# Four weight pieces reach bf16 inside their transfers instead of through a staging tile and a cast

## The chip, the cores and the metric

The kernel runs on one core of one Trainium2 chip. Its time is the device time of one execution in microseconds (us). Three executions of the kernel before took 511.12, 511.17 and 511.69 us, the median being 511.17 us. One further execution was recorded by the hardware profiler, and all rows shown below come from it.

The core has five engines with a queue of instructions each, which run in the order of the program and meet only at semaphores: PE (TensorE, matrix products; PEld is its loading of weights), DVE (VectorE), ACT (ScalarE), POOL (GpSimd) and SP (SyncE, which here only issues transfers). 16 DMA engines move the data between HBM and the on-chip memory.

## The reference, cut to what matters

The input is a sequence of 4 x 5824 tokens with 256 channels. A gated linear recurrence runs along each sequence, and a feed-forward part follows it:

```python
sig_r, sig_i = sigmoid(r_gate), sigmoid(i_gate)
a = exp(8 * sig_r * log(sigmoid(a_param)))         # decay per token and channel
u = sqrt(max(1 - a*a, 1e-6)) * sig_i * x
h[t] = a[t] * h[t-1] + u[t]                        # within each of the 4 sequences
out = ((h @ w1) * (h @ w2)) @ w3 @ w_out           # w1, w2: 256x1024, w3: 1024x1024, w_out: 1024x256
```

All inputs and the output are float32. The matrix products run in bf16 with float32 sums.

## The kernel before, in words

The 23,296 tokens are cut into 47 chunks: two of 256 tokens, 44 of 512 and one of 256. Channels lie on the 128 partitions in two blocks, tokens along the free dimension. For each chunk the gates are loaded (r, i, x), pass through the activation function (R, I), are turned from token rows to channel rows (V, U) by PE or by a transposing transfer, and become the decay a (d), its square and root (s, q), the gated input (g), the scan (h) and its bf16 copy y (y). Then come the products with the first up weight w1 (step a) and the second up weight w2 (step b), their evacuation and elementwise product (c, m), and the product with the folded weight (D), its evacuation (e) and the store (o).

w3 and w_out meet no nonlinearity between them, so the kernel folds them once into one 1024x256 weight: each of the eight row blocks of w3 is cast to bf16 (Cw3.k), turned by PE (Ftk), copied out of PSUM (Fck), multiplied with the whole of w_out (Fmk), and scaled into the folded weight (Fek).

All weights are float32 in HBM and bf16 on chip. In the kernel before each piece of 512 KB is loaded by SP's queue into a float32 staging tile named wf (step L, line 407), which takes a slot in the rings of tiles of a or nrm, and is cast by an engine (step C, lines 414 and 416) into its bf16 tile: w_sb for w1 and w2 (two pieces each, Lw2.0 being columns 0 to 511 of w2), wo_sb for w_out (two pieces, Lwo.0 being its first four row blocks), w_t for a block of w3. `W_ACT` and `W_DVE` name the pieces that ACT and DVE cast, POOL casts the others. The function `load_w` has a second way already, for the pieces in the set `CASTING`, which is empty in the kernel before: the transfer is issued on POOL's queue (line 404), straight from float32 HBM into the bf16 tile, and it has no step C.

The order of the whole program is written out by hand, in a table of words (`ORDER`). Each word issues one step, and each engine's own order follows from the order of the words. W is a group of filler products on PE which keep its clock up at the start; they are in the table like all else. SP's transfers share eight completion semaphores in turn, so an issue on SP waits for the transfer issued eight before it. Transfers on POOL's queue have semaphores of their own, which order prints as DMASW0, DMASW1 and so on in the order of their issue. Names of rows: thi or i_t is the i gate after its activation; p2 is the step L173 on POOL (1 + tanh), t2 the step L192 (times x, into u_t), U2 the turning of u_t by PE (L200), g2 the step L248 on DVE, h the scan (L270), y the cast of h (L280, L282).

Of the kernel before, what the change touches and what calls it, by code (L numbers as in the profile page):

```python
# [23 lines left out]
def kernel(  # L24
# [74 lines left out]
    W_DVE = {('w1', 1)}  # L99
    STAGE = {'w1': ['a', 'a'], 'w2': ['nrm', 'nrm'], 'w3': ['a', 'nrm', 'a', 'nrm', 'a', 'nrm', 'a', 'nrm'], 'wo':  # L100
        ['a', 'nrm']}
    CASTING = set()
    WARM = [2] * 16
    HALVED = 4
    RINGS = {"r": 4, "i": 5, "x": 4, "th_r": 3, "u": 2, "rt": 2, "ut": 6, "a": 6, "nrm": 6, "h": 2, "y": 4,
# [277 lines left out]
    def piece(nm, i):  # L383
        if nm in ("w1", "w2"):
            cols = slice(i * CT, (i + 1) * CT)
            w_in, w_sb = (moe_w1, w1_sb) if nm == "w1" else (moe_w2, w2_sb)
            return w_in.rearrange("(cb p) f -> p cb f", p=P)[:, :, cols], w_sb[:, :, cols]
        if nm == "wo":
            ks = slice(4 * i, 4 * i + 4)
            return moe_w_out.rearrange("(ko p) f -> p ko f", p=P)[:, ks, :], wo_sb[:, ks, :]  # L390
        return moe_w3[i * P:(i + 1) * P, :].rearrange("p (k f) -> p k f", k=1), None
# [7 lines left out]
    def load_w(nm, i):  # L399
        if (nm, i) in CASTING:  # L400
            dst = piece(nm, i)[1]
            if dst is None:
                T["w3b", i] = dst = ring(ffn, [P, 1, DFF], BF16, name="w3_t", tag="w3")
            nc.gpsimd.dma_start(out=dst, in_=piece(nm, i)[0])
            return
        T["wf", nm, i] = ring(held, [P, NCB, CT], F32, name="wf", tag=STAGE[nm][i])
        nc.sync.dma_start(out=staged(nm, i), in_=piece(nm, i)[0])  # L407
# [66 lines left out]
    def last(c):  # L474
# [18 lines left out]
    }  # L493

    ORDER = """
        r0 i0 x0 Lw1.1 Lw1.0 r2 i2 Lw2.0 Lw3.2 x2 E W13 A3. A0. A1. A2. R0.1 R0.0 W3 W10 V0.0 V0.1 I0 t0.1 d0.0 s0.0
        d0.1 s0.1 q0.0 t0.0 Cw1.1 q0.1 Cw1.0 R2 I2 W5 W8 W0 U0 W4 W11 W6 W12 W7 W9 W2 g0 h0.1 h0.0 y0.1 y0.0 a0.0.1
        a0.1.1 a0.1.0 a0.0.0 V2 W15 Cw2.0 g1 h1.1 h1.0 y1.1 y1.0 d2.1 Lw2.1 Lwo.1 Lwo.0 r3 Cw3.2 d2.0 s2.1 s2.0 q2
        b0.0 c0.0.0 c0.1.0 a1.1.0 m0.0 Ft2 a1.1.1 c1.1.0 b0.1 a1.0.0 a0.2.1 a1.0.1 b1.1 m0.1 Fc2 b1.0 a0.2.0 p2 t2.0
        t2.1 U2 c1.0.0 m1.1 Cw2.1 m1.0 a0.3.1 W14 b0.2 a1.3.1 W1 a1.3.0 c0.2.0 g2 Cwo.1 Cwo.0 r4 Lw3.0 Lw3.5 i3 Lw3.1  # L500
        Lw3.4 x3 Lw3.3 Lw3.6 Lw3.7 r7 m0.2 h2.0 h2.1 R3 a1.2.1 a1.2.0 a0.3.0 c1.3.0 c0.3.0 Fm2 b0.3 b1.2 V3 R4 V4
        c1.2.0 d3.1 d4.0 d3.0 d4.1 m0.3 b1.3 y2 Fe2 m1.2 m1.3 a2.0.0 a2.0.1 b2.0 a2.1.0 c2.0.1 c2.0.0 c2.1.0 m2.0
        Cw3.0 s3.1 Cw3.5 Cw3.1 b2.1 a2.2.1 Ft0 a2.1.1 Fc0 Ft1 c2.1.1 Fc1 s4.0 I3 s4.1 c2.2.1 a2.2.0 Ft5 Fm0 p3 Cw3.4
# [161 lines left out]
```

## Time and profile before

| | kernel before |
|---|---|
| device time, median of 3 | 511.17 us (511.12 to 511.69) |
| profiled execution: span from the first to the last instruction | 509.1 us |
| what lies around that span, against the median | 2.07 us |
| granted TensorE clock | 1.000 |
| PE busy | 501.7 us (99%) |
| ACT / DVE / POOL busy | 461.5 / 431.8 / 318.0 us |
| DMA queues with data | q1 (SP), 123.50 MB; q10, below 0.01 MB |

The page gives no device time of the profiled execution by itself, only its span; sums below are made against the span and carried to the median with the 2.07 us unchanged. "Idle before" in a row is the idle time of that engine just before the row's first instruction, and what released it. A merged row of x4 covers four instructions. PE's rows overlap one another a little, since products are pipelined.

### The profile page before, as it was taken

How to read it: one execution, taken by the hardware profiler on the slowest of the kernel's cores; microseconds unless marked ns; L12 is line 12 of the kernel's file. 1: busy time of each engine (PE TensorE's matmuls, PEld its weight loads, DVE VectorE, ACT ScalarE, POOL GpSimd, SP SyncE). 2: the span in 40 equal slices, each digit the busy share in tenths (PEclk: the TensorE clock that was granted, in tenths of full speed). 3: DMA queues.
4: the chain of work that ended last, by engine and by line, in shares of the span. 5: the costliest groups of instructions: out<-in, count | busy, mean ns of one | idle time of the engine just before them, and what ended most of it. 6: DMA issues, size and time to landing. Idle time of an engine off the chain costs nothing.

```text
span 509.1 us, 8891 instructions
## 1 busy us (share of the span) xinstructions
PE 501.7 (99%) x3225; PEld 308.3 (61%) x3225; DVE 431.8 (85%) x417; ACT 461.5 (91%) x708; POOL 318.0 (62%) x269
## 2 busy tenths in 40 slices
PE   7999999999999999999999999999999999999997
PEld 3767665665665656556656556565566655656566
DVE  6999999999999789879979799878877797959762
ACT  7999999998999999999999999998998979888543
POOL 1686677658658937964886973956647568580200
PEclk9999999999999999999999999999999999999999
DMA  8999999999989998896999997899886895252213
GB/s 317 410 411 345 335 316 282 305 286 259 310 220 298 279 285 247 211 302 196 247 305 327 254 286 148 252 243 227 210 246 164 235 298 161 85 166 62 65 51 104
DMA packets 178048, 124.06 MB, mean 244 GB/s; under 512 B 87378, under 2 KB 174036, under 8 KB 178004
## 3 DMA queue, kind: packets, MB, share of 16 engines
q1 hardware_dynamic: 178000, 123.50, 85.4%
q8 instruction: 25, 0.41, 0.4%
q14 instruction: 19, 0.16, 0.1%
q10 hardware_dynamic: 4, 0.00, 0.0%
HBM read 78.91 MB, written 23.86 MB: 202 GB/s over the span
## 4 chain that ended last, share of the span: by engine, by line
PE 92%; ACT 3%; DMA 2%; POOL 1%; DVE 1%; issue 1%; SPq 1%; ACTq 0%; DVEq 0%
PE po L357 30%; PE pb L299 29%; PE pa L299 29%; DMA wf<-in_moe_w_dram 2%; PE pw L436 1%; ACT sa L322 1%; PE ptr L200 1%; PE ptw L425 1%; POOL u_t L192 0%; DVE h_t L270 0%; SPq L151 0%; ACT ot L322 0%; SPq L407 0%; ACT L168 0%; ACT L238 0%
## 5 line engine op out<-in xcount | busy, mean ns | idle before, releaser
L337 DVE TENSOR_TENSOR g_t<-sa,pb 128x1024 bf16<-128x1024 bf16 (+1 forms) x188 | 218.7, 1180 | 58.9 <-PE pb L299 27.6
L299 PEld LDWEIGHTS <-w_sb 128*128 128x128 bf16 x1504 | 146.4, 98 | 144.1 <-issue 1.4
L322 ACT CAST sa<-pa 128x512 bf16<-128x512 f32 (+1 forms) x332 | 179.8, 591 | 27.1 <-PE pa L299 18.9
L299 PE MATMUL pa<-y_t,w_sb 128*128 128x512 bf16 (+1 forms) x752 | 190.2, 372 | 0.2 <-ACT sa L322 0.2
L299 PE MATMUL pb<-y_t,w_sb 128*128 128x512 bf16 (+1 forms) x752 | 184.9, 372 | 0.2 <-ACT w_sb L414 0.2
L357 PE MATMUL po<-wp_sb,g_t 128*128 128x256 bf16 (+1 forms) x1464 | 177.6, 272 | 0.0
L357 PEld LDWEIGHTS <-g_t 128*128 128x128 bf16 x1464 | 142.5, 98 | 39.5 <-issue 0.3
L282 POOL CAST y_t<-h_t 128x1024 bf16<-128x1024 f32 (+2 forms) x47 | 53.8, 1145 | 140.2 <-DVE h_t L270 136.1
L192 POOL TENSOR_TENSOR u_t<-i_t,x_t 128x512 bf16<-128x512 f32 (+1 forms) x90 | 123.3, 1387 | 3.8 <-DMA ut<-u_t 1.8
L270 DVE TENSOR_TENSOR_SCAN h_t<-a_t,h_t,nrm 128x512 f32<-128x512 f32 (+1 forms) x92 | 121.1, 1343 | 1.6
L233 POOL TENSOR_TENSOR nrm<-a_t 128x512 f32<-128x512 f32 x70 | 78.4, 1137 | 7.0 <-ACT a_t L223 4.0
L223 ACT ACTIVATE a_t<-rt,la 128x512 f32<-128x512 bf16 (+1 forms) x82 | 66.1, 823 | 0.0
L322 ACT COPY ot<-po 128x512 f32<-128x512 f32 x84 | 49.1, 589 | 13.2 <-PE po L357 12.9
L173 POOL TENSOR_SCALAR i_t<-i_t 128x1024 f32<-128x1024 f32 (+1 forms) x45 | 55.4, 1233 | 8.3 <-ACT i_t L168 8.3
L251 DVE SCALAR_TENSOR_TENSOR nrm<-nrm,ut 128x1024 f32<-128x1024 f32 (+1 forms) x39 | 53.2, 1365 | 5.2 <-ACT nrm L238 5.2
L168 ACT ACTIVATE i_t<-i_t 128x1024 f32<-128x1024 f32 (+1 forms) x46 | 48.5, 1063 | 0.3 <-DMA i_t<-in_i_gate_dram 0.2
L238 ACT ACTIVATE nrm<-nrm 128x1024 f32<-128x1024 f32 (+1 forms) x47 | 48.4, 1040 | 0.2
L162 ACT ACTIVATE th_r<-r_t 128x1024 bf16<-128x1024 f32 (+1 forms) x41 | 43.5, 1064 | 0.0
L320 DVE CAST sa<-pa 128x512 bf16<-128x512 f32 x36 | 23.5, 684 | 1.4 <-PE pa L299 0.8
L238 ACT ACT_TABLE_LOAD x17 | 21.8, 1283 | 0.4
L287 PE MATMUL warm<-ident 128*128 128x512 bf16 x32 | 10.7, 473 | 1.6 <-DVE ident L441 1.6
L231 ACT ACTIVATE nrm<-a_t 128x512 f32<-128x512 f32 x18 | 11.4, 645 | 0.0
(55 smaller groups left out, 122.1 us busy)
## 6 DMA issues: line engine op xcount, KB each, us to landing
r_t<-in_r_gate_dram SPq DMA_DIRECT2D x45, 512.0 KB, 5.2
i_t<-in_i_gate_dram SPq DMA_DIRECT2D x45, 512.0 KB, 6.0
x_t<-in_x_dram SPq DMA_DIRECT2D x45, 512.0 KB, 5.5
out_dram<-ot SPq DMA_DIRECT2D x90, 256.0 KB, 3.9
wf<-in_moe_w_dram SPq DMA_DIRECT2D x12, 512.0 KB, 10.5
wf<-in_moe_w_out_dram SPq DMA_DIRECT2D x2, 512.0 KB, 10.2
rt<-th_r SPq DMA_TRANSPOSE x41, 4.7
ut<-u_t SPq DMA_TRANSPOSE x39, 4.4
```

Source lines behind the costliest of these rows:

```text
L173: (nc.vector if c in DV_PLUS else nc.gpsimd).tensor_scalar(t, t, 1.0, 1.0, op0=ALU.add, op1=ALU.mult)
L192: (nc.vector if (c, half) in DV_HALF else nc.gpsimd).tensor_mul(out=u, in0=t, in1=xt)
L223: nc.scalar.activation(out=a, in_=pr, func=AF.Exp, scale=la4[:, cb:cb + 1], bias=la4[:, cb:cb + 1])
L233: (nc.vector if (c, cb) in DV_SQUARE else nc.gpsimd).tensor_mul(out=n, in0=a, in1=a)
L238: nc.scalar.activation(out=n, in_=n, func=AF.Sqrt, scale=-1.0, bias=1.0)
L251: nc.vector.scalar_tensor_tensor(out=n, in0=n, scalar=1e-3, in1=T["pu", c][:, :, cols], op0=ALU.max, op1=ALU.mult)
L270: nc.vector.tensor_tensor_scan(h[:, cb, :], a[:, cb, :], n[:, cb, :], init, ALU.mult, ALU.add)
L282: (nc.vector if key in DV_CAST else nc.gpsimd).tensor_copy(out=y, in_=h)
L299: nc.tensor.matmul(out=dst, lhsT=w_sb[:, cb, m * P:(m + 1) * P], rhs=T["y", gates_of(c)][:, cb, span(c, mp)], start=(cb == 0), stop=(cb == ...
L322: nc.scalar.copy(out=dst, in_=src_ps)
L337: nc.vector.tensor_mul(out=T["g", z][:, 2 * mp:2 * mp + 2, span(c, mp)], in0=T["sa", c, mp][:, :, :w], in1=T["pb", c, mp][:, :, :w])
L357: nc.tensor.matmul(out=po, lhsT=T["g", c][:, k, j * P:(j + 1) * P], rhs=wp_sb[:, k, cols], start=(k == 0), stop=(k == KD - 1), skip_group_ ...
```

## The change

The set `CASTING` now holds both pieces of w2 and both of w_out. Their loads leave SP's queue and are issued by POOL, and the four casts (one on ACT, three on POOL) are gone with their staging tiles. In the table, Lw2.0 moves from its place between i2 and Lw3.2 to a place behind Cw1.0, and the words of the four casts are taken out; Lw2.1, Lwo.1 and Lwo.0 stay where they were.

```diff
-    CASTING = set()
+    CASTING = {('w2', 0), ('w2', 1), ('wo', 0), ('wo', 1)}
...
     ORDER = """
-        r0 i0 x0 Lw1.1 Lw1.0 r2 i2 Lw2.0 Lw3.2 x2 E W13 A3. A0. A1. A2. R0.1 R0.0 W3 W10 V0.0 V0.1 I0 t0.1 d0.0 s0.0
-        d0.1 s0.1 q0.0 t0.0 Cw1.1 q0.1 Cw1.0 R2 I2 W5 W8 W0 U0 W4 W11 W6 W12 W7 W9 W2 g0 h0.1 h0.0 y0.1 y0.0 a0.0.1
-        a0.1.1 a0.1.0 a0.0.0 V2 W15 Cw2.0 g1 h1.1 h1.0 y1.1 y1.0 d2.1 Lw2.1 Lwo.1 Lwo.0 r3 Cw3.2 d2.0 s2.1 s2.0 q2
+        r0 i0 x0 Lw1.1 Lw1.0 r2 i2 Lw3.2 x2 E W13 A3. A0. A1. A2. R0.1 R0.0 W3 W10 V0.0 V0.1 I0 t0.1 d0.0 s0.0
+        d0.1 s0.1 q0.0 t0.0 Cw1.1 q0.1 Cw1.0 Lw2.0 R2 I2 W5 W8 W0 U0 W4 W11 W6 W12 W7 W9 W2 g0 h0.1 h0.0 y0.1 y0.0 a0.0.1
+        a0.1.1 a0.1.0 a0.0.0 V2 W15 g1 h1.1 h1.0 y1.1 y1.0 d2.1 Lw2.1 Lwo.1 Lwo.0 r3 Cw3.2 d2.0 s2.1 s2.0 q2
         b0.0 c0.0.0 c0.1.0 a1.1.0 m0.0 Ft2 a1.1.1 c1.1.0 b0.1 a1.0.0 a0.2.1 a1.0.1 b1.1 m0.1 Fc2 b1.0 a0.2.0 p2 t2.0
-        t2.1 U2 c1.0.0 m1.1 Cw2.1 m1.0 a0.3.1 W14 b0.2 a1.3.1 W1 a1.3.0 c0.2.0 g2 Cwo.1 Cwo.0 r4 Lw3.0 Lw3.5 i3 Lw3.1
+        t2.1 U2 c1.0.0 m1.1 m1.0 a0.3.1 W14 b0.2 a1.3.1 W1 a1.3.0 c0.2.0 g2 r4 Lw3.0 Lw3.5 i3 Lw3.1
```

On POOL, the place is the first stage, from the cast of w1's first piece on. Before, its rows were:

```order
L416 CAST w_sb<-wf 128x2x512
L282 CAST y_t<-h_t 128x256 x2
L416 CAST w_t<-wf 128x1024
L173 TENSOR_SCALAR i_t<-i_t 128x1024
L192 TENSOR_TENSOR u_t<-i_t,x_t 128x512 x2
L416 CAST w_sb<-wf 128x2x512
L416 CAST wo_sb<-wf 128x1024 x2
L282 CAST y_t<-h_t 128x1024
```

And with the change:

```order
L416 CAST w_sb<-wf 128x2x512
L404 DMA w_sb<-in_moe_w_dram 128x2x512
L282 CAST y_t<-h_t 128x256 x2
L404 DMA w_sb<-in_moe_w_dram 128x2x512
L404 DMA wo_sb<-in_moe_w_out_dram 128x4x256 x2
L416 CAST w_t<-wf 128x1024
L173 TENSOR_SCALAR i_t<-i_t 128x1024
L192 TENSOR_TENSOR u_t<-i_t,x_t 128x512 x2
L282 CAST y_t<-h_t 128x1024
```

Three casts behind t2 are gone. One issue now stands ahead of the two casts of chunk 0's y, and three stand ahead of the cast of w3's block 2 (Cw3.2), of p2 and of t2.

On PE the order of rows is the same; what they wait for is not. These are the first product with w2 (b0.0), and the first product with w_out (Fm2):

```order
 L287 MATMUL warm<-ident 128x512
-L299 LDWEIGHTS w_sb [waits Activation_49]
+L299 LDWEIGHTS w_sb [waits DMASW0_49]
 L299 MATMUL pb<-y_t,w_sb 128x256 [waits PE_49]
 L299 LDWEIGHTS w_sb
```

```order
 L299 MATMUL pa<-y_t,w_sb 128x256
-L436 LDWEIGHTS w3t [waits DVE_49]
-L436 MATMUL pw<-wo_sb,w3t 128x256 [waits Pool_49]
+L436 LDWEIGHTS w3t [waits DMASW3_49]
+L436 MATMUL pw<-wo_sb,w3t 128x256 [waits DVE_49]
 L436 LDWEIGHTS w3t
```

b0.0 waits for the landing of the first transfer on POOL's queue where it waited for ACT's cast, and Fm2 for the fourth (w_out's first half) where it waited for POOL's cast.

On SP, four loads leave the early part of the queue:

```order
 L151 DMA i_t<-in_i_gate_dram 128x1024
-L407 DMA wf<-in_moe_w_dram 128x2x512
 L407 DMA wf<-in_moe_w_dram 128x1024
 L151 DMA x_t<-in_x_dram 128x1024
-L407 DMA wf<-in_moe_w_dram 128x2x512
-L407 DMA wf<-in_moe_w_out_dram 128x4x256 x2
 L151 DMA r_t<-in_r_gate_dram 128x1024 x2
```

The load of w3's block 2 and that of chunk 2's x now stand one load further ahead, all that follows four loads further.

## The prediction

> **What bounds the kernel now.** I read three views in this order: the page's shares, the busy time by stage, and the chain of waits at the start. The page makes PE the bound, but an average doesn't say whether a late start is caught up again, so the table by stage comes next. Its columns are the stretch, its length, then busy time and count of PE, PEld, DVE, ACT and POOL, the granted clock, the DMA share and GB/s:
>
> ```profile
> PE 501.7 (99%) x3225; PEld 308.3 (61%) x3225; DVE 431.8 (85%) x417; ACT 461.5 (91%) x708; POOL 318.0 (62%) x269
> ...
> 14.00:15.22 1.22, 1.03 (x13) 0.54 (x10) 1.22 (x3) 1.10 (x2) 0.00 (x0) 1.00 1.00 408
> 15.22:22.00 6.78, 5.89 (x56) 4.61 (x57) 5.99 (x11) 6.74 (x9) 6.54 (x7) 1.00 1.06 402
> 22.00:495.30 473.30, 473.11 (x3006) 288.69 (x3005) 411.90 (x373) 438.38 (x674) 308.69 (x254) 1.00 0.87 243
> ```
>
> From 22 us to 495 us PE stands idle for 473.30 - 473.11 = 0.19 us. Whatever reaches PE late before 22 us therefore moves the end by the same amount, and nothing behind has room to give it back; nor can work saved on ACT or POOL there help. The change works before 22 us only: there PE's idle time from 14 us on is 0.19 + 0.89 = 1.08 us, and that is all that can be won. The rows of PE say where it lies (start, length, engine, line, what, and in brackets the idle time before it); POOL's follow:
>
> ```profile
> 15.22 0.61 PE L299 MATMUL pb<-y_t,w_sb 128*128 128x256 bf16 x4 [0.19 <-ACT w_sb L414]
> 15.67 0.38 PE L299 MATMUL pa<-y_t,w_sb 128*128 128x256 bf16 x2
> 16.47 0.62 PE L425 MATMUL ptw<-ident,w_t 128*128 128x128 bf16 x8 [0.43 <-POOL w_t L416]
> 19.34 0.28 PE L200 MATMUL ptr<-ident,u_t 128*128 128x128 bf16 x2
> 20.07 0.51 PE L200 MATMUL ptr<-ident,u_t 128*128 128x128 bf16 x6 [0.46 <-POOL u_t L192]
> 23.04 1.04 PE L436 MATMUL pw<-wo_sb,w3t 128*128 128x256 bf16 x8
> 26.38 1.02 PE L299 MATMUL pa<-y_t,w_sb 128*128 128x512 bf16 x4
> ```
> ```profile
> 10.35 1.04 POOL L416 CAST w_sb<-wf 128x1024 bf16<-128x1024 f32 x1 [9.04 <-DMA wf<-in_moe_w_dram]
> 11.99 1.06 POOL L282 CAST y_t<-h_t 128x256 bf16<-128x256 f32 x2 [0.61 <-DVE h_t L270]
> 15.38 1.04 POOL L416 CAST w_t<-wf 128x1024 bf16<-128x1024 f32 x1 [2.33 <-DMA wf<-in_moe_w_dram]
> 17.52 2.50 POOL L192 TENSOR_TENSOR u_t<-i_t,x_t 128x512 bf16<-128x512 f32 x2
> 19.97 1.03 POOL L416 CAST w_sb<-wf 128x1024 bf16<-128x1024 f32 x1
> 20.95 2.02 POOL L416 CAST wo_sb<-wf 128x1024 bf16<-128x1024 f32 x2
> 25.28 1.04 POOL L282 CAST y_t<-h_t 128x1024 bf16<-128x1024 f32 x1 [2.32 <-DVE h_t L270]
> ```
>
> PE's waits at 15.22, 16.47 and 20.07 all end with a cast of weights or with POOL. The chain of waits (start, length, what) names one path for the last two:
>
> ```profile
> 4.66 10.66 DMA wf<-in_moe_w_dram
> 15.32 0.05 issue
> 15.38 1.04 POOL w_t L416
> 16.42 1.03 POOL i_t L173
> 17.45 0.07 issue
> 17.52 2.51 POOL u_t L192 x2
> 20.03 0.05 issue
> 20.07 0.51 PE ptr L200 x6
> 20.58 0.22 PE pa L299 x2
> ```
>
> So the start is set by POOL: the load of w3's block 2 lands at 15.32, then Cw3.2, p2 and t2 run back to back to 20.03, and PE goes on at 20.07. Ahead of that, POOL is idle twice, for 0.61 and for 2.33 us, together 2.94 us. The change puts four issues into these gaps.
>
> **What goes, and what it is worth.** Three POOL casts, 1.03 and 2.02 us in the rows above, stood behind t2 and before y2 at 25.28, which waited 2.32 us for the scan anyway: removing them is worth nothing there.
>
> ```profile
> 14.12 1.04 ACT L414 CAST w_sb<-wf 128x1024 bf16<-128x1024 f32 x1 [0.22 <-DMA wf<-in_moe_w_dram]
> 20.64 0.59 PE L287 MATMUL warm<-ident 128*128 128x512 bf16 x2
> 21.05 0.56 PEld L299 LDWEIGHTS <-w_sb 128*128 128x128 bf16 x6 [0.31 <-POOL w_sb L416]
> ```
>
> The weight load that waited 0.31 us for w2's second piece did so while PE ran filler products (20.64 to 21.23), so nothing is won there either. ACT's cast of w2.0, 1.04 us, gives way to b0.0's own wait for the transfer; ACT is up to 1.04 us earlier, but what it computes next goes to g2, which waits for U2 too. SP loses four loads. The one row that waited for SP's order is Cw3.2: its load now stands one load further ahead.
>
> **The price of an issue on POOL, g.** No row has a transfer issued by POOL. The nearest are SP's plain loads and its transposing transfers, which write many small pieces (least, median and greatest duration, ns):
>
> ```profile
> L407 SPq DMA_DIRECT2D wf<-in_moe_w_dram x12: 327/368/496, 2.1 to 25.0; - x12
> L211 SPq DMA_TRANSPOSE rt<-th_r x41: 1210/1307/2977, 40.3 to 446.0; - x41
> ```
>
> That bounds g by 0.33 us and 1.31 us. I take 1.0 us, nearer the upper row, since each issue covers 256 or 512 rows of the weights, and what is slow in the upper row is a transfer of many pieces. An issue can't be free of POOL's order, since POOL runs it as an instruction between two casts.
>
> Term A, POOL's order. Cw1.0 ends at 10.35 + 1.04 = 11.39. Then come an issue, the y casts (1.06), three issues, and Cw3.2 to t2's end (20.03 - 15.38 = 4.65). t2 ends at 11.39 + 1.06 + 4.65 + 4g = 17.10 + 4g, against 20.03: a shift of 4g - 2.93. With g = 1.0 it is +1.07 us, with 1.31 +2.31. With 0.33 the formula gives -1.61, but then the landing of w3's block 2 and PE's idle time bound it. Queued behind are Cw3.2, p2 and t2 on POOL, Ft2 and U2 on PE, and g2, the scan and y2. y2 ends at 25.28 + 1.04 = 26.32, just ahead of PE's next products at 26.38: nothing there absorbs it. The y casts of chunk 0 start at 12.39 instead of 11.99; the products behind them are 0.40 us late, less than b0.0 by term B.
>
> Term B, the landing of w2.0. How long does a transfer of 512 KB take from the end of its issue? The first load meets empty engines:
>
> ```profile
> 0.74 0.39 SPq L151 DMA_DIRECT2D r_t<-in_r_gate_dram  x1
> 4.29 1.15 ACT L160 ACTIVATE th_r<-r_t 128x512 bf16<-128x512 f32 x2 [0.81 <-DMA r_t<-in_r_gate_dram]
> wf<-in_moe_w_dram SPq DMA_DIRECT2D x12, 512.0 KB, 10.5
> ```
>
> That is 4.29 - 1.13 = 3.16 us alone. But between 14 and 22 us the engines' share is 1.00 and over, at 408 GB/s, by which 512 KB cost 1.28 us of all engines. The lower bound is the load alone: 11.39 + 1.0 + 3.16 = 15.55. The upper is a transfer that stands behind all that SP has in flight, as SP's weight loads do, 10.5 us: 12.39 + 10.5 = 22.9. I take an equal share between two queues that both hold work, which doubles 1.28: 16.83. b0.0, at 15.22 before, starts at 16.88, 1.66 us late. PE's wait of 0.43 us for Cw3.2 and part of the next then vanish, and Ft2 stands at 17.55 (16.88 + 0.67 for the six products ahead of it: 15.67 - 15.22 = 0.45, and 0.22 for the two by the chain's last row); Cw3.2 ends at 11.39 + 4.0 + 1.06 + 1.04 = 17.49. So B and A meet, and the shift at U2 stays +1.07.
>
> One sentence of the Trainium skill bears on B: DMA: Bandwidth & Descriptors, section Issuing engines are not separate DMA queues, states that transfers of all issuing engines interleave on the same 16 DMA engines, which gives the equal share and not the 22.9; no run so far has two busy queues to show it. Another page of the Trainium skill speaks against the change: SBUF — State Buffer, section SBUF: two separate sides, states that VectorE in a two-port mode, such as a float32 copy within SBUF, keeps GpSimd from writing descriptors. Between 11.39 and 16.45 this trace has one such row on DVE, so by that rule the sum would grow by 0.27 us at most:
>
> ```profile
> 14.50 0.27 DVE L282 CAST y_t<-h_t 128x256 bf16<-128x256 f32 x1
> ```
>
> Term C, the landing of w_out. Fm2 needs the fourth transfer on the queue. At an equal share each of the four takes 2.56 us behind the last, so it lands at 16.83 + 3 x 2.56 = 24.51; alone, 3.16 us after its issue at 16.45, it would be 19.6. Fm2, at 23.04 before, stands at 24.11 by A. It waits 0.45 us more, since PE has no idle time behind to lose: +1.07 + 0.45 = +1.52. w2.1, second on the queue, lands at 19.4, before its use at 22.2.
>
> The sum is 509.1 + 1.5 = 510.6 us of span, and with the 2.07 us around it 512.7 us.
>
> **The rivals.**
>
> Cheap issue. If g is like SP's row, 0.33 to 0.5 us, POOL is no longer late: with 0.4 the issues end at 11.39 + 1.6 + 1.06 = 14.05, the load of w3's block 2 lands one load earlier, 15.32 - 1.28 = 14.04, and t2 ends at 18.7. PE then is held by w2.0 alone, at 11.39 + 0.4 + 3.16 = 14.95 to 16.2 by its share: b0.0 up to 1.0 us late, against 0.89 us of idle time behind it that falls away. With 16.2 it is +0.1, 511.3 us; with 14.95 it is -0.9, 510.3 us. For it: SP's rows. Against it: SP's issue is work for an engine that does nothing else. The Trainium skill, DMA: Bandwidth & Descriptors, section Latency and other measured facts, has about 1 us to the first byte on GpSimd's path and about 0.6 us on SP's; by that ratio SP's 0.33 to 0.5 would be 0.55 to 0.83 us, and term A -0.7 to +0.4, an estimate.
>
> Price by rows. If an issue costs by the rows it names, w2's 256 at 1.0 us and w_out's 512 at 2.0, the four take 6.0 us and A is 17.10 + 6.0 - 20.03 = +3.1: 514.2 us. The landings are then later by less than that. For it: the transposing transfers at 1.31 against 0.37 us. Against it: a load's issue of 512 KB shows no such growth on SP.
>
> Late landing. Transfers on POOL's queue come behind SP's backlog, or move slower because they convert. Then B decides, from a landing of about 17 us on: at 22.9 b0.0 is 7.7 us late, less 0.89 of idle time, +6.8: 518.0 us. For it: DMA engines full at 14 us. Against it: the queues are separate, and SP issues no more than eight transfers ahead.
>
> That the new transfers don't convert, or that the casts remain, is excluded: the order of rows shows four issues and four casts fewer.
>
> **How the numbers follow.** Forecast (+0.9 to +2.4) 0.40; price by rows (+2.4 to +5) 0.21; late landing 0.08; cheap issue 0.31, of which 0.06 reach below 510.1, since the idle time to be won is only 1.08 us. The measurement can tell 0.2%, here 1.02 us, from no change: slower is 0.36 of the forecast, the two dear rivals, and 0.01 of the cheap one, together 0.66; the same 0.28; faster 0.06. The range takes in g from about 0.5 us and issues by rows with a slow share: 510.5 to 516.5. It leaves out the far end of the late landing and the best of the cheap issue.
>
> **What would show it.** POOL's rows: y casts of chunk 0 at 12.4, Cw3.2 starting at 16.45 without a wait for its load, t2 ending at 21.1. PE: b0.0 waiting for w_sb until 16.9, U2 for u_t until 21.15, Fm2 for wo_sb until about 24.5, and again no idle time from there to 495 us. If Cw3.2 starts before 15.4, the issue was cheap and A is wrong; if it starts past 18, it goes by rows; if b0.0 waits past 17.5 while POOL is in time, it is the landing. A shift at U2 that the end does not show would make the first step wrong, that nothing behind 22 us gives time back.

## The result, and the profile after

The changed kernel takes 527.25 us (median of 4, 526.99 to 527.93) beside 511.38 us for the kernel before (511.12 to 511.69): a ratio of 1.0313, 95% interval 1.0298 to 1.0327. It is slower by 15.9 us, where the prediction had 512.7 us and a range that ended at 516.5. The profiled execution took 527.13 us with a span of 525.3 us, 16.2 us more than the span before.

The table of stages, in the same columns as before:

```profile
15.22:22.00 6.78, 2.14 (x14) 1.44 (x13) 3.45 (x5) 5.13 (x7) 4.95 (x5) 0.67 1.10 335
29.05:37.06 8.01, 0.02 (x1) 0.00 (x0) 2.01 (x2) 2.22 (x4) 2.02 (x2) 0.63 1.12 356
37.06:42.26 5.20, 5.20 (x36) 4.17 (x37) 1.62 (x3) 0.66 (x1) 0.00 (x0) 0.58 1.05 398
42.26:511.50 469.24, 466.16 (x2910) 285.19 (x2963) 407.32 (x366) 434.41 (x669) 305.44 (x251) 1.00 0.84 228
```

PE stands still twice, and around and after each stop the granted clock (the third number from the end) is below 1. From 42.26 us on the kernel is the old one: the stretch there takes 469.24 us, and the same work before, from the first product at 26.38 us to 495.30, took 468.92. (PE's busy time there looks 3.1 us short of the stretch, but the trace holds 2910 products where the one before held 2961, so records are missing.) The tail behind it is 13.8 us in both. So the whole loss arises before 42.26 us. PE's rows name the two stops:

```profile
20.19 1.03 PE L299 MATMUL pb<-y_t,w_sb 128*128 128x256 bf16 x4 [4.64 <-DMA w_sb<-in_moe_w_dram]
28.03 1.04 PE L299 MATMUL pa<-y_t,w_sb 128*128 128x256 bf16 x8
37.06 1.89 PE L436 MATMUL pw<-wo_sb,w3t 128*128 128x256 bf16 x8 [7.99 <-DMA wo_sb<-in_moe_w_out_dram]
42.26 1.03 PE L299 MATMUL pa<-y_t,w_sb 128*128 128x512 bf16 x3
```

The first product with w2 waits for its transfer until 20.19 (15.22 before), the first with w_out until 37.06 (23.04 before). At 42.26 the same product stands that stood at 26.38. The 16.2 us divide so: PE reaches the end of the products ahead of Fm2 at 37.06 - 7.99 = 29.07 instead of 23.04, 6.0 us late through w2; then 8.0 us of waiting for w_out; then the products from Fm2 on take 5.20 us instead of 3.34 (26.38 - 23.04), 1.9 us; and 0.3 us behind. These are the parts of PE's path and not separate causes: Fm2 starts when w_out has landed at 37.0, and PE's first 6.0 us only shorten its wait for that. POOL, on which the sum rested, is nearly in time:

```profile
11.26 0.93 POOL L404 DMA_DIRECT2D w_sb<-in_moe_w_dram  x1
12.36 1.05 POOL L282 CAST y_t<-h_t 128x256 bf16<-128x256 f32 x2 [0.18 <-DVE h_t L270]
13.35 0.72 POOL L404 DMA_DIRECT2D w_sb<-in_moe_w_dram  x1
14.07 1.51 POOL L404 DMA_DIRECT2D wo_sb<-in_moe_w_out_dram  x2
15.55 1.07 POOL L416 CAST w_t<-wf 128x1024 bf16<-128x1024 f32 x1
17.77 2.48 POOL L192 TENSOR_TENSOR u_t<-i_t,x_t 128x512 bf16<-128x512 f32 x2
```

The issues take 0.93, 0.72 and twice 0.76 us, and t2 ends at 20.25 us, 0.2 us later than before. What is late is the transfers, not their issue. The view of the DMA queues shows why, for 16 to 18 us and for 26 to 28 us (packets, MB as written, busy share of the 16 engines):

```profile
q1 hardware_dynamic: 142, 0.52, 68.7%
q0 software_dynamic: 144, 0.15, 43.2%
...
q1 hardware_dynamic: 165, 0.61, 82.0%
q0 software_dynamic: 164, 0.08, 30.4%
```

q1 is SP's queue, q0 POOL's. In each stretch both queues move the same number of packets: 142 and 144, 165 and 164. But a packet of SP's carries 0.52 MB / 142 = 3.7 KB, one of POOL's 1.0 KB written (a row of 2 KB of w2, converted), and with w_out 0.5 KB (a row of 1 KB). The engines take turns packet by packet, so POOL's queue gets half of the turns and, counted at the source, 0.15 x 2 = 0.3 of 0.8 MB with w2, and 0.16 of 0.77 MB with w_out. A row of w2 has its turn every 2 x 16 / 144 = 0.22 us on each engine, and a piece has 16 rows for each engine: 3.6 us; a piece of w_out has 32, at 0.195 us: 6.2 us. The Trainium skill, DMA: Bandwidth & Descriptors, section Queues, rings and completion order, states the rule, that each engine goes round between the queues by whole packets; these rows agree with it.

### The profile page after: what moved, and what is told of

Same layout as the page of the kernel before. It is cut to its first block, busy times and chain, and to the rows that moved or that the text cites. A ratio compares the mean times of both kernels' runs of the same rounds, so it can differ in the third digit from the quotient of the medians.

```text
span 525.3 us, 8830 instructions
## 1 busy us (share of the span) xinstructions
PE 503.2 (96%) x3170; PEld 311.3 (59%) x3225; DVE 433.6 (83%) x417; ACT 460.7 (88%) x707; POOL 317.9 (61%) x270
## 3 DMA queue, kind: packets, MB, share of 16 engines
q1 hardware_dynamic: 176400, 121.40, 82.4%
## 4 chain that ended last, share of the span: by engine, by line
PE 88%; DMA 5%; ACT 3%; DVE 1%; issue 1%; POOL 0%; SPq 0%; DVEq 0%; ACTq 0%
PE po L357 29%; PE pb L299 29%; PE pa L299 27%; DMA wo_sb<-in_moe_w_out_dram 4%; PE pw L436 2%; ACT sa L322 1%; DMA x_t<-in_x_dram 1%; PE ptr L200 1%; PE ptw L425 1%; DVE h_t L270 1%; ACT ot L322 0%; DVE u_t L189 0%; ACT L168 0%; ACT L238 0%; DVE nrm L233 0%
## 5 line engine op out<-in xcount | busy, mean ns | idle before, releaser
L299 PE MATMUL pa<-y_t,w_sb 128*128 128x512 bf16 (+1 forms) x719 | 186.2, 373 | 1.1 <-ACT sa L322 0.2
L233 POOL TENSOR_TENSOR nrm<-a_t 128x512 f32<-128x512 f32 x70 | 78.4, 1137 | 16.2 <-ACT a_t L223 15.4
L436 PE MATMUL pw<-wo_sb,w3t 128*128 128x256 bf16 x64 | 9.0, 291 | 8.0 <-DMA wo_sb<-in_moe_w_out_dram 8.0
L223 ACT ACTIVATE a_t<-ptr,la 128x512 f32<-128x512 bf16 x10 | 7.2, 774 | 10.4 <-issue 10.3
```

What stands on the lines that cost most here:

```text
L223: nc.scalar.activation(out=a, in_=pr, func=AF.Exp, scale=la4[:, cb:cb + 1], bias=la4[:, cb:cb + 1])
L233: (nc.vector if (c, cb) in DV_SQUARE else nc.gpsimd).tensor_mul(out=n, in0=a, in1=a)
L299: nc.tensor.matmul(out=dst, lhsT=w_sb[:, cb, m * P:(m + 1) * P], rhs=T["y", gates_of(c)][:, cb, span(c, mp)], start=(cb == 0), stop=(cb == ...
```

## The experiments

Theory T is these turns: two queues with work share the engines packet for packet, and what a queue gets in bytes goes by the size of its packets. Its rivals are that converting is slow by itself, that POOL's queue delivers slowly whatever else runs, and that one piece alone is at fault. "Before" was timed beside every run; the ratios below have their 95% interval behind them.

### Which piece costs what

```diff
w2_only
-    CASTING = {('w2', 0), ('w2', 1), ('wo', 0), ('wo', 1)}
+    CASTING = {('w2', 0), ('w2', 1)}          # w_out loaded by SP and cast by POOL as before
wo_only
+    CASTING = {('wo', 0), ('wo', 1)}          # w2 loaded by SP and cast as before
```

> Only the two pieces of w2 are converted in transfers on POOL's queue; w_out is loaded by SP and cast by POOL as before. Theory T (each DMA engine serves the two queues packet by packet, one for one, and POOL's packets are single rows): w2.0 lands at about 20, w2.1 at about 24, as in the changed kernel, Fm2 waits for nothing; PE stays about 6 us late after U2 and the time is about 517 us. Rival C (converting is what is slow, w_out's half included): the same landing of w2. Rival S (one cause only, w_out's late landing, decides, and the wait at b0.0 is absorbed): no change, 511 to 512 us.

> Only the two pieces of w_out are converted in transfers on POOL's queue; w2 is loaded by SP and cast by ACT and POOL as before. Theory T: 64 rows for each engine at one turn in about 0.21 us, from about 15 us on, so the second transfer lands at about 28.5; Fm2 starts there instead of 23.0, and with a lower clock behind the wait the time is 517 to 518 us. Rival S: the whole 16 us come from here, 525 us or more. If the issues alone cost, 512 us.

w2 alone: 515.49 us against 511.21, 1.0084 (1.0067 to 1.0101), +4.3 us. w_out alone: 521.44 us, 1.0204 (1.0187 to 1.0221), +10.2 us. The two don't have to add up to the 15.9 us, since all four transfers stand in one queue. Each piece has its own wait on PE:

```profile
19.36 1.03 PE L299 MATMUL pb<-y_t,w_sb 128*128 128x256 bf16 x4 [4.22 <-DMA w_sb<-in_moe_w_dram]
```
```profile
31.58 1.89 PE L436 MATMUL pw<-wo_sb,w3t 128*128 128x256 bf16 x8 [8.43 <-DMA wo_sb<-in_moe_w_out_dram]
```

The first row is of the kernel with w2 alone, the second of that with w_out alone. Both pieces are at fault, and rival S falls. The sizes were off: w2 costs 1.5 us less than forecast, and w_out lands at 31.5 instead of 28.5, because I let its rows start at 15 us. POOL's queue shows no packet before 17 us there, though its first issue ended at 14.1.

### Is it converting, and is it the queue?

The same four transfers, at the same places on POOL's queue but unconverted, with the casts of before:

```diff
plain_pool (against before; Lw2.0 moved as in the change)
-        nc.sync.dma_start(out=staged(nm, i), in_=piece(nm, i)[0])
+        (nc.gpsimd if nm in ('w2', 'wo') else nc.sync).dma_start(out=staged(nm, i), in_=piece(nm, i)[0])
```

> The same four transfers on POOL's queue at the same places, but not converted: float32 into the staging tiles, cast by ACT and POOL as before. Theory T: packets on POOL's queue stay single rows, the landings are like the changed kernel's (20, 24, 31, 37 us), the casts come on top and stand in POOL's order ahead of y2: 528 us or more. Rival C (converting is what is slow): unconverted transfers get a share by bytes like SP's own, w2.0 lands at 16 to 17, w_out at 24 to 25, and the time is 513 to 516 us.

It takes 517.51 us, 1.0121 (1.0106 to 1.0136): better than the changed kernel, with four casts more. From 20 to 22 us its queues stand so, and over the run q0 has:

```profile
q1 hardware_dynamic: 115, 0.43, 52.9%
q0 software_dynamic: 113, 0.40, 48.9%
```
```profile
q0 software_dynamic: 576, 2.10, 1.0%
```

The turns are one for one again, but the bytes are equal too. 576 packets for 2.10 MB are 3.6 KB each: 512 of them are what packets of 4 KB for each piece and partition give, and the other 64 are 16 for each transfer. So unconverted, POOL's queue joins the rows of one partition (two of w2, four of w_out) into a packet, where the changed kernel has 1600 packets for the same source. So I was wrong that its packets stay single rows, and rival C is right in that converting makes a difference. w2.0 lands at 18.7, w_out's last piece at 27.4, between the two forecasts. PE waits only for the first: b0.0 starts at 19.80. Is converting slow, then, or only its packets small? The next kernel takes SP's packets away:

```diff
quiet (against the change)
+        T["r", 3] = ring(loads, [P, 4, D], F32, name="r_t", tag="r")
+        nc.gpsimd.tensor_copy(out=T["r", 3][:, 0, 0:1], in_=wo_sb[:, 0, 0:1])   # ahead of SP's load r3
```

> The changed kernel, but SP's queue is held: its load of chunk 3's r waits, by one element that POOL copies out of w_out's last piece into that tile, until all four transfers of POOL's queue have landed. SP has then only four loads in flight beside them, and none from about 16 us on. The time means nothing here, the landings do. Theory T (turns): without the other queue's turns a row of w2 takes about 0.10 us of an engine and a row of w_out 0.06, so w2.0 lands by 18 to 19 and w_out's last piece by 23 to 25. Rival L (POOL's queue brings a row each 0.2 us by itself, whatever else runs): 20, 24, 31 and 37 us as in the changed kernel.

From 18 to 20 us only POOL's queue runs, and POOL's copy begins when the last of the four has landed:

```profile
q0 software_dynamic: 738, 0.37, 135.6%
...
20.87 0.19 POOL L420 CAST r_t<-wo_sb 128x1 f32<-128x1 bf16 x1 [5.88 <-DMA wo_sb<-in_moe_w_out_dram]
```

738 packets in 2 us instead of 164, and all landed by 20.9 us instead of 37.0, earlier than the 23 to 25 of the forecast: a row of w_out took 2 x 16 / 738 = 0.043 us of an engine and not 0.06. This kernel ran once, and only its landings are used. Of w_out's rows that is 738 x 1 KB = 0.76 MB of source in 2 us, 378 GB/s, beside the 408 GB/s of plain loads: converting itself is nearly as fast as loading. Rival L falls, and so does slow converting by itself. What is left is the size of its packets beside SP's.

### Longer rows

w2 by row blocks and w_out with eight neighbouring rows on a partition, so that a row of the transfer is 4 KB; the turning of w3 takes its columns in the matching order:

```diff
long_rows (against the change)
+        if nm == "w2":
+            return moe_w2[i * P:(i + 1) * P, :], w2_sb[:, i, :]
-            return moe_w_out.rearrange("(ko p) f -> p ko f", p=P)[:, ks, :], wo_sb[:, ks, :]
+            return moe_w_out.rearrange("(p ko) f -> p ko f", p=P)[:, ks, :], wo_sb[:, ks, :]
-            nc.tensor.matmul(out=pt[:, k, :], lhsT=T["w3b", mi][:, 0, k * P:(k + 1) * P], rhs=ident,
+            nc.tensor.matmul(out=pt[:, k, :], lhsT=T["w3b", mi][:, 0, :].rearrange("p (q k) -> p k q", k=KD)[:, k, :], rhs=ident,
```

> The changed kernel with the same bytes in fewer, longer rows: w2 by row blocks (128 rows of 4 KB a piece, where it was 256 of 2 KB) and w_out with eight neighbouring rows on a partition (128 rows of 4 KB a piece, where it was 512 of 1 KB; the columns of w3 are turned in the matching order). Theory T: 32 turns for each engine in all, where it was 96; b0.0 now needs both pieces of w2, at about 19 to 20; w_out lands by 26, before Fm2 needs it at 28 to 29; 516 to 517 us. Rival C by bytes: the landings stay as they are and b0.0, which needs both pieces, starts at 24: 527 us or more.

518.06 us, 1.0134 (1.0119 to 1.0149): of 15.9 us 9 are gone. The queues from 16 to 18 us, and PE's only waits from there to 45 us:

```profile
q1 hardware_dynamic: 115, 0.44, 57.9%
q0 software_dynamic: 109, 0.19, 50.4%
```
```profile
18.35 0.39 PE L299 MATMUL pb<-y_t,w_sb 128*128 128x256 bf16 x1 [3.30 <-DMA w_sb<-in_moe_w_dram]
20.92 0.82 PE L299 MATMUL pb<-y_t,w_sb 128*128 128x256 bf16 x3 [2.17 <-DMA w_sb<-in_moe_w_dram]
```

0.19 MB written are 0.38 MB of source beside 0.44: with packets of like source size the queues share alike. Fm2 waits no more. What is left is b0.0, which here needs both pieces, the second at 20.9 instead of the 19 to 20 forecast, and the time is 1 us above the 516 to 517 forecast. With w_out alone in long rows (w2 as before):

> Only w_out is converted on POOL's queue, with 128 rows of 4 KB a piece; w2 as before. Theory T: 16 turns for each engine, landed by 21 to 22, before Fm2 at 23.0; the two issues (1.5 us) fit into POOL's idle 2.33 us: 511.2 us, no change. Rival C by bytes: like the run with w_out in short rows.

512.28 us against 511.43, 1.0017 (1.0009 to 1.0026), +0.85 us where +10.2 was the price in short rows. The miss against "no change" is one wait, since w_out lands at 24.0 and not at 21 to 22:

```profile
24.07 1.05 PE L436 MATMUL pw<-wo_sb,w3t 128*128 128x256 bf16 x8 [0.73 <-DMA wo_sb<-in_moe_w_out_dram]
```

Even then there is no gain: the casts saved were covered.

### A second queue that needs no POOL

```diff
plain_act (against before; Lw2.0 moved as in the change)
+        (nc.scalar if nm in ('w2', 'wo') else nc.sync).dma_start(out=staged(nm, i), in_=piece(nm, i)[0])
```

> The same four transfers, unconverted, issued by ACT instead of POOL at the same places, cast as before. Theory T: ACT's queue forms packets of some 3.7 KB as SP's does, so that turns one for one are an equal share of bytes: w2.0 lands at 15 to 17, w_out by 25; 511 to 515 us. If any second queue gets little beside SP's (a rival to the size of packets): landings like the changed kernel's and 525 us or more.

527.89 us, 1.0322 (1.0306 to 1.0339): as slow as the change, and my forecast was wrong by more than 12 us. Its queues from 14 to 16 us and from 28 to 30 us, q10 being ACT's:

```profile
q1 hardware_dynamic: 146, 0.53, 65.1%
q10 hardware_dynamic: 143, 0.29, 38.7%
...
q1 hardware_dynamic: 176, 0.64, 78.5%
q10 hardware_dynamic: 176, 0.18, 25.5%
```

The turns are equal once more. I had taken it that ACT's queue joins rows as I thought SP's did; it does not: its packets are the rows, 2 KB and 1 KB. Nor did SP's queue join them: it has 178,000 packets before and 176,400 in the changed kernel, 1600 fewer for the same four transfers. SP's packets are large in this stage because its rows are (4 KB of w3, and of the r, i and x of chunks 2, 3, 4 and 7). The rival that any second queue gets little has the time right, 525 us or more, but not the cause: in plain_pool POOL's queue got as many bytes as SP's. This kernel is no pure test of the queue, for its issues also stand in ACT's order:

```profile
18.52 3.71 ACTq L407 DMA_DIRECT2D wf<-in_moe_w_out_dram  x2
22.28 0.78 ACT L223 ACTIVATE a_t<-ptr,la 128x512 f32<-128x512 bf16 x1 [3.15 <-DMA wf<-in_moe_w_dram]
```

ACT stands idle for 3.15 us ahead of the row at 22.28, around its second issue of w_out, and the issue of w2.1 comes only at 18.11, behind ACT's cast of w2.0 (on POOL it came at 13.35). So q10 moves 48 packets from 16 to 18 us, none from 18 to 20 and 28 from 20 to 22; at 72 packets per us (143 in 2 us) its queue moved next to nothing for about 4.9 us, an estimate of what ACT's order adds to the landing of w_out at 36.8. The rest of that landing is the turns; no run separates the two.

### The clock

```diff
warm (against the change)
-    WARM = [2] * 16
+    WARM = [2] * 15 + [24, 18, 18]
-        ... a0.3.0 c1.3.0 c0.3.0 Fm2 ...
+        ... a0.3.0 c1.3.0 c0.3.0 W16 W17 Fm2 ...
```

> The changed kernel with filler products on PE where it waits: 22 more ahead of b0.0 (4.7 us) and 36 ahead of Fm2 (7.7 us), sized to end about when the transfers land. Theory: the landings stay, but the granted clock stays at 1.0 through the waits, so the products from 37 to 42 us run at full pace and the time falls by about 2 us to 525 us. Rival (the clock costs nothing, the whole 16 us are waits): no change, or slower by the fillers.

525.02 us, ratio 1.0264 (1.0250 to 1.0278) where the change had 1.0313: 2.2 us less, by products that compute nothing. Behind the landing of w_out, its row and that of the change stand so:

```profile
37.00:42.20 5.20, 5.15 (x45) 3.81 (x46) 3.38 (x6) 2.77 (x5) 1.91 (x2) 1.00 1.05 397
```
```profile
37.06:42.26 5.20, 5.20 (x36) 4.17 (x37) 1.62 (x3) 0.66 (x1) 0.00 (x0) 0.58 1.05 398
```

With fillers the clock is 1.00 and PE issues 45 products in the time of 36. Before the change the same stage, and in the changed kernel the first stretch behind each stop, stand so:

```profile
23.04:26.38 3.34, 3.33 (x39) 2.89 (x37) 3.34 (x5) 3.34 (x7) 1.10 (x2) 1.00 1.02 419
```
```profile
20.19:24.00 3.81, 3.81 (x22) 2.94 (x23) 1.56 (x3) 0.67 (x1) 0.07 (x1) 0.50 1.10 334
37.06:41.00 3.94, 3.94 (x22) 2.96 (x23) 1.09 (x3) 0.00 (x0) 0.00 (x0) 0.50 1.05 404
```

For nearly 4 us behind each stop the clock is half. A wait of PE thus costs more than its length. Behind the first stop the loss is hidden in the wait for w_out, so what the fillers win is the loss behind the second.

### Could the transfers be put elsewhere?

```diff
hold_sp (against the change): ahead of SP's load r3
+        nc.sync.dma_start(out=held_t, in_=wo_sb[0:1, 0, 0:2])
early (against before): Lw2.0 as the first transfer of POOL's queue, the other pieces as before
+    CASTING = {('w2', 0)}
-        r0 i0 x0 Lw1.1 Lw1.0 r2 i2 Lw2.0 Lw3.2 x2 ...
+        Lw2.0 r0 i0 x0 Lw1.1 Lw1.0 r2 i2 Lw3.2 x2 ...
```

> The changed kernel, but SP's queue has one tiny transfer that reads one row of w_out's last piece ahead of its load of chunk 3's r, so that SP issues no more loads until the four transfers of POOL's queue have landed, and no engine but SP waits for that. If turns taken by SP's packets are what made the landings late, w2.0 lands at 16.9 and w_out at 20.4, as when the queue was held by POOL; U2 ends about 1 us later than before the change, Fm2 waits for nothing; but chunk 3's r lands at about 24 instead of 22, so PE gets V3 up to 1.5 us late: 512.5 to 514.5 us in all. If something else made them late, 520 us or more.

> Only w2.0 is converted in a transfer, and it is issued by POOL as its first transfer at about 1 us, where POOL is idle until 10.3; the other three pieces are loaded and cast as before. By turns it lands at 9 to 10 us, ahead of its use at 15.2, so no product waits for it. But its 16 rows for each engine take turns from the loads of chunk 0 (x, w1), which are up to 1.5 us late, and with them the first y; the load of w3's block 2 lands when it did. 511.3 to 512.5 us. If the missing cast on ACT were worth something, 510.3 us or less.

With SP held, w2.0 is there at 16.7 us and Fm2 waits for nothing, as forecast, yet the kernel takes 516.98 us, 1.0105 (1.0090 to 1.0120), above the forecast of at most 514.5. ACT waits 2.11 us for chunk 3's r:

```profile
25.51 1.06 ACT L160 ACTIVATE th_r<-r_t 128x1024 bf16<-128x1024 f32 x1 [2.11 <-DMA r_t<-in_r_gate_dram]
60.00:100.00 40.00, 39.03 (x261) 24.23 (x259) 37.80 (x39) 39.85 (x59) 27.01 (x22) 1.00 1.14 314
```

The load is 1.5 us later than I had it. At the product that stands at 26.38 before, this kernel is 3.1 us late (29.43), but its span is 6.6 us longer (515.7 against 509.1), so half of the loss arises behind this stage. From 60 to 100 us PE loses 0.97 us that it did not lose before, at a DMA share of 1.14 where it was 1.07. I take it that SP's loads had a lead and lost it here; no run shows that. Issued first of all, w2.0 lands 9.2 us after its issue at 1.28, at about 10.5 instead of the 9 to 10 forecast, and no product waits for it. The kernel takes 513.05 us, 1.0031 (1.0018 to 1.0044), +1.4 us and 0.5 above the forecast: chunk 0's x and w1, which share their turns with it, come later, and POOL's cast of w1 starts at 12.30 instead of 10.35. No version tried is faster than the kernel before.

## Why the prediction was wrong, point by point

**That PE's idle time before 22 us bounds a gain, and that nothing behind gives time back**: right. From the same product on, the changed kernel takes 0.3 us more than before, and no kernel tried was faster. Time can still be lost there, as with SP held.

**The price of an issue, 1.0 us** (term A): a little high. It took 0.93 us for the first and 0.72 to 0.76 for the others, 3.2 us for the four instead of 4.0, so t2 ended at 20.25 us instead of 21.1, and the shift from POOL's order was +0.2 us, not +1.07. The rival "price by rows" fell: 512 rows cost no more than 256 (0.76 and 0.72 us; in the kernel with long rows 128 rows took 0.54).

**"I take an equal share between two queues that both hold work, which doubles 1.28: 16.83"** (term B): this is the step that failed. The queues do share equally, but by packets. At 3.7 KB against a converted row a piece of w2 takes 3.6 us and not 2.56, and its first packet comes only some 3.5 us after the end of the issue (12.19 to about 15.7, by the 23 packets that it moved before 16 us), where I had taken 3.16 us from issue to landing without a second queue. w2.0 landed at 20.1, 3.3 us past the value taken, between my bounds of 15.55 and 22.9. It is the case that I had named under what would show it: b0.0 waits past 17.5 while POOL is in time, so it is the landing.

**"Each of the four takes 2.56 us behind the last"** (term C): the same error, larger, since w_out's rows are 1 KB: 6.2 us a piece. Its last piece landed at 37.0 instead of 24.5, and the wait of 0.45 us became 7.99. For this term, which decided, I had worked out no upper bound at all.

**The rival "late landing"** had the right place, a landing past 17 us, and 0.08 of the chance. Its price came from w2 alone, 6.8 us, and its mechanism, a queue behind SP's backlog or slow conversion, is not what the runs show: while both queues have work, their packets alternate, and held apart from SP's packets the same transfers landed by 20.9 us. Only for the 3.5 us ahead of the first packet does a backlog stay open: in quiet 12 packets had moved by 14 us, at most 2 us after the end of the issue at 12.01. The sentence of the Trainium skill on interleaving (DMA: Bandwidth & Descriptors, section Issuing engines are not separate DMA queues), which I set beside B, is borne out by the equal counts; the step from equal turns to equal bytes was mine.

**The clock** was in no term. It adds about 2 us behind the wait for w_out, by the run with fillers.

**The rule of the Trainium skill on VectorE's two-port mode, +0.27 us at most** (SBUF — State Buffer, section SBUF: two separate sides): not seen. In the changed kernel DVE's cast of y starts at 15.60, when the last issue has ended at 15.58, so it is no test; in quiet the cast starts at 14.27, beside an issue, and the issues take the same (0.92, 0.72 and 1.51 us for two). It is DVE that was slowed (below), and in the changed kernel not on the path, as b0.0 came later still.

## What to carry to other kernels

Where a second queue is put to work while the DMA engines are full, count packets and not bytes: its share of bytes goes by the size of its packets beside the other queue's, and a converting transfer sent one packet for each row here. Give such a transfer long rows, or a stage in which the engines are not full, and sum up the landing of the last transfer on the queue as well as of the first. Before an engine's cast is moved into a transfer, look whether the cast was on the path at all; here it saved nothing where it was hidden, and a late weight stops PE, whose clock was half for nearly 4 us behind each stop.

## What the runs showed of the hardware that I had not expected

A converting transfer moves its source nearly as fast as a plain load (378 beside 408 GB/s when alone), but loses by packets in company. POOL's queue joins rows of 1 and 2 KB to 4 KB when it doesn't convert (576 packets), ACT's (1604, of which 4 are there before too) and SP's (1600) don't for the same transfers.

DVE's cast of y grows beside casts and arithmetic on POOL. Before, with POOL idle, it took 0.27 us. Its row in the changed kernel, and below it that in the kernel with fillers (warm):

```profile
15.60 1.19 DVE L282 CAST y_t<-h_t 128x256 bf16<-128x256 f32 x1
```
```profile
14.56 2.93 DVE L282 CAST y_t<-h_t 128x256 bf16<-128x256 f32 x1
```

The first ends at 16.79, just after POOL's cast of w3 (15.55 to 16.62), the second at 17.49, just after POOL's p2 (16.28 to 17.34). In all seven kernels where this cast takes over 1 us, it ends 0.15 to 0.17 us after a row of POOL's; in the five others, with 0.27 to 0.34 us, POOL has no cast or arithmetic under way when it starts. In hold_sp it takes 2.93 us too and is on the path: PE waits 0.21 us for it at 17.67, a part of that kernel's miss. That POOL's rows hold it is an inference from these times, as no run was made to separate it. It is not the whole account: where it takes 2.93 us it starts beside POOL's last issue, as it does at 14.27 in quiet, where it takes 0.27.

Chunk 1's scans also grew in the changed kernel, from 1.39 to 2.13 us for the two:

```profile
13.54 2.13 DVE L270 TENSOR_TENSOR_SCAN h_t<-a_t,h_t,nrm 128x256 f32<-128x256 f32 x2
```

They run beside POOL's issues from 13.35 to 15.58, but in warm they take 1.39 us beside the same issues, so the issues alone are not the cause; it stays open.
